# Joins of two chunks in one PSUM tile, over all four 32-row parts, with the Gram products in the same runs (DeltaNet and maxout FFN, one core)

## The chip, the cores and the metric

The kernel runs on one core of one Trainium2 chip. The time is the device time of one execution in microseconds. A core has a matrix engine (TensorE, in the profile PE for matmuls and PEld for weight loads), a vector engine (VectorE, DVE), a scalar engine (ScalarE, ACT), GpSimd (POOL) and a queue that mainly starts DMA transfers (SyncE, SP). Matmuls write to PSUM; DVE and ACT move results from there to SBUF, and here that is called an evacuation.

## What is computed

A delta-rule attention over four batches and eight heads, followed by a feed-forward layer that takes the largest of three products:

```python
k_n = k / (np.linalg.norm(k, axis=-1, keepdims=True) + 1e-06)
for t in range(S):
    kt, vt, bt = (k_n[:, :, t], v[:, :, t], beta[:, :, t, None])
    y[:, :, t] = np.einsum('bhd,bhde->bhe', q[:, :, t], state)
    v_old = np.einsum('bhde,bhd->bhe', state, kt)
    state = state + bt[:, :, :, None] * np.einsum('bhd,bhe->bhde', kt, vt - v_old)
...
x = attn_out.transpose(0, 2, 1, 3).reshape(B * S, H * D)
h = np.maximum(np.maximum(x @ w1, x @ w2), x @ w3)
return h @ w_out
```

B, H, S, D are 4, 8, 768, 48; x is 3072 x 384, w1 to w3 are 384 x 768, w_out is 768 x 384. All inputs are fp32.

## The kernel before

**Chunks, units, groups.** The sequence is cut into 12 chunks of 64 positions. A unit is a chunk of two of the four batches (`n = 2 * c + g`), so there are 24 units; a group is four units, or two chunks, or 512 tokens of the FFN, and there are six. The FFN of group m (`ffn(m)`, L1150) runs while the attention of group m + 1 is made. The order is written by hand: `ffn(m)` is a generator, and after each of its steps `links(m + 1, ...)` (L1348) issues the small pieces of work that the table `LINKS` (L1317) names for this step. A name is a letter and a number: `g` Gram products of a unit, `z` and `j` the two joins of a chunk, `d` transposes for the second join, `k` and `q` products with the state, `u` the new values, `s` the state's update, `y` and `x` outputs, `t` transposed keys and queries, `N` and `L` loads of them. `EARLY_LINKS` is the table for group 1 beside `ffn(0)`, and `FIRST` has the second chunk of group 0. Group 0's first chunk is issued ahead of all (L1283 to L1311).

**Gram products.** `gram(n)` (L395) multiplies keys by keys and queries by keys of a unit into a PSUM tile `p_g`. DVE masks the query part into `pt` (L390), then ACT copies the key part into `at` (L423), and `to_dram` (L427) sends `at` to DRAM with four DMAs, on SP in most groups and on POOL's queue for units 10 and 11.

**Solve.** For each group, `blocks` (L478) loads the 32 x 32 diagonal blocks back (`x_bl`), and `solve` (L498) inverts all of them at once on DVE: after norms (a square root on ACT, L261, into `root_bl`, then small DVE instructions from L262), 31 pairs of DVE instructions (L552, L556) in `x_bl` and `y_bl`. The result goes through DRAM to `ut` (L577, L586).

**Joins.** A chunk of 64 has two blocks of 32. The corner of the inverse is minus the product of the first inverse, the block between and the second inverse. `join_z(c)` (L694) multiplies `at` by the second inverse: for each of 8 heads four matmuls of 32 x 32 by 32 (`TILES`, two partition halves by two units), from rows 32 to 63 and 96 to 127 to PSUM rows 0 to 31 and 64 to 95. Two ACT copies of 32 x 512 bring it to `z` (L705). `join_u(c)` (L707) multiplies the transposed first inverse `t1` by `z`, and two ACT multiplications by -1 write the corner into `ut` (L716). For chunk 0 the heads are split in two batches, with one of four evacuations of `join_u` on DVE (`heads_of`, `negated_of`). `turn_t1` (L615) makes `t1` with DVE transposes. Chunk 0 and 1 have a finer split of the inverse before the joins (`halves_z`, `halves_u`).

**After the joins.** `old_k` subtracts the state's part from v, `new(c)` (L753) multiplies by `ut` into `p_u` and copies to `u`, `step` updates the state `st`, `to_y` makes the output.

**FFN.** A step `hidden` of `ffn(m)` is three matmuls of 128 x 128 by 512 columns into `p_h` (L1161), evacuated by ACT (L1171, L1169) or by DVE as a maximum (L1175); the PSUM tiles of the FFN have two buffers. fp32 matmuls stand in the trace as two records each. The small work shares a PSUM ring of three tiles of two banks (`ps_two`, L83). `weights()` (L221) converts the FFN's weights in `ffn(0)`: three ACT instructions (L238 to L240), one of DVE (L250), one of POOL (L254), with two buffers. `both_layers` (L891) adds matmuls `p_m` in `ffn(1)`.

Of the kernel before, what the change touches and what calls it, by code (L numbers as in the profile page):

```python
# [16 lines left out]
C = 64  # L17
DP = 64
BL = 32
# [4 lines left out]
def kernel(  # L24
# [31 lines left out]
    nc = tc.nc  # L56

    B, H, S, D = q.shape
# [9 lines left out]
    NK, NQ, NU = 8, 3, 2  # L68
# [14 lines left out]
    def ps_two(name):  # L83
        return psum.tile([128, 2, 512], FP32, name=name, tag="two", bufs=3)
# [220 lines left out]
    kqts, ats, pts, xs, at_d = {}, {}, {}, {}, {}  # L305
# [42 lines left out]
    def load_blocks(n, queue=nc.gpsimd):  # L348
        c, g = divmod(n, 2)
        for i in range(2):  # L350
            if n % 4 == 2:
                t = kmore[i].rearrange("p a h d -> p (a h d)")[:, 0 : 2 * TURNED]
                t = t.rearrange("p (b x) -> p b x", b=2)
            else:
                t = work.tile(
                    [128, 2, TURNED], FP32, name="turned", tag="w_bits", bufs=5
                )
            turned[n, i] = t
            nc.gpsimd.memset(t[:, :, TURNED - 48 : TURNED], 0.0)  # L359
# [35 lines left out]
    def gram(n, parts=(0, 1), queues=one_queue, copy=nc.scalar.copy, later=False):  # L395
        kqt, g = kqts[n], n % 2
        p_g = ps_two("p_g")

        whole = len(parts) == 2 and not g
        for j in range(NP):  # L400
            for par in range(2):
                for bb in range(2):
                    kq = kqt[dims(par), j, bb ^ g]
                    for i in (0,) if whole else parts:
                        c0 = j * 128 + i * C
                        nc.tensor.matmul(  # L406
                            p_g[
                                rows(bb ^ (g * i)), par, c0 : c0 + C * (1 + whole)
                            ],
                            kq[:, 0],  # L410
                            kq if whole else kq[:, i],
                        )
        p_v = p_g.rearrange("p two (j i t) -> p two j i t", j=NP, i=2)
        if 1 in parts:
            pt = pts[n] = square("pt")
            if later:
                copy(by_par(pt), p_v[:, :, :, 1])
            else:
                masked(pt, p_v[:, :, :, 1])
        if 0 not in parts:  # L420
            return
        at = ats[n] = square("at")
        copy(by_par(at), p_v[:, :, :, 0])  # L423
        if queues:
            to_dram(n, queues)
# [186 lines left out]
    def block(bb, f=0, n=BL):  # L612
        return slice(C * bb + BL * f, C * bb + BL * f + n)
# [47 lines left out]
    def span(hs):  # L661
        return slice(hs[0], hs[-1] + 1)
# [28 lines left out]
                        -1.0,  # L691
                    )

    def join_z(c):  # L694
        at = [ats.pop(2 * c + g) for g in range(2)]
        z, second = zs[c % NU], ut[c % NU][:, :, :, BL:C]
        for hs, p_v, _ in heads_of(c, "p_z", BL):
            for i, h in enumerate(hs):
                for bb, g in TILES:
                    r = block(bb, 1)  # L700
                    nc.tensor.matmul(
                        p_v[block(bb ^ g), g, i], at[g][r, h, 0:BL], second[r, g, h]
                    )
            for bb in range(2):
                nc.scalar.copy(z[block(bb), :, span(hs)], p_v[block(bb)])  # L705

    def join_u(c):  # L707
        z, t = zs[c % NU], t1[c % NU]
        u12 = ut[c % NU][:, :, :, BL:C]
        for hs, p_v, negate in negated_of(c, "p_j", BL):  # L710
            for i, h in enumerate(hs):
                for bb, g in TILES:
                    r = block(bb ^ g)
                    nc.tensor.matmul(p_v[bb][block(bb), g, i], t[r, g, h], z[r, g, h])  # L714
            for bb in range(2):
                negate[bb](u12[block(bb), :, span(hs)], p_v[bb][block(bb)], -1.0)  # L716


    xts, rhss, qss, us, yts = {}, {}, {}, {}, {}
# [595 lines left out]


    LINKS = {  # L1317
# [3 lines left out]
    }  # L1321
    LAST_LINKS = {**LINKS, 17: "", 19: "X1"}
    EARLY_LINKS = {
# [3 lines left out]
    }  # L1327

# [7 lines left out]

    RECURS = dict(
        z=join_z, j=join_u, k=old_k, q=old_q, u=new, s=step, y=to_y, x=to_x,
        e=halves_z, f=halves_u, d=turn_t1,
    )  # L1340
    MADE = dict(V=load_v, P=prep_values)
    UNIT = dict(
        t=turn, K=load_k, L=lambda n: load_blocks(n, nc.sync),
        g=lambda n: gram(n, queues=(nc.gpsimd,) * 2 if n in (10, 11) else one_queue),
# [129 lines left out]
```

## Time and profile before

| | |
|---|---|
| runs | 510.63, 512.64, 512.75 us; median 512.64 |
| span of the profiled execution, first to last instruction (the page gives no other time of it) | 510.5 us |
| PE busy | 491.1 us (96%) |
| DVE busy | 349.9 us (69%) |
| POOL busy | 192.7 us (38%) |
| ACT busy | 168.7 us (33%) |
| join matmuls, L701 and L714 | 768 records each, 9.1 and 10.4 us |
| their evacuations, L705 and L716 | 26 on ACT; 25 on ACT and one on DVE |
| mean granted TensorE clock | 0.966; 0.57 from 20 to 45 us |

A matmul's record lasts from its start to its modelled end, and matmuls overlap, so busy time is not work at full rate; starts and the chain of waits say more. The granted clock of PE is 1.00 from 55 us on. Busy time by stretch, from the windows of the trace (us, PE, DVE, ACT, POOL busy):

| stretch | what runs | PE | DVE | ACT | POOL |
|---|---|---|---|---|---|
| 20 to 45 | first chunk | 19.17 | 22.14 | 18.62 | 10.62 |
| 55 to 74 | ffn(0), chunk 1 | 16.88 | 17.61 | 14.31 | 9.14 |
| 104 to 116 | ffn(0), group 1 | 12.00 | 7.45 | 11.36 | 9.36 |
| 116 to 131 | ffn(0), group 1 | 13.91 | 14.38 | 4.30 | 4.75 |
| 242 to 315 | ffn(2) | 73.00 | 48.68 | 17.14 | 43.49 |
| 315 to 359 | ffn(3) | 43.91 | 24.71 | 14.45 | 13.41 |

### The profile page before, as it was taken

To read this page: it belongs to the slowest core of one execution; us is meant where nothing else is said; L and a number is where in the kernel's file an instruction comes from. 1 tells how busy PE (TensorE), PEld (TensorE's weight loads), DVE (VectorE), ACT (ScalarE), POOL (GpSimd) and SP (SyncE) were. 2 spreads that over 40 slices of the span, in tenths; PEclk is the share of its full clock that TensorE was granted. 3 is DMA by queue.
4 is the path that set the end of the run, shared out by engine and by line. 5 is a ranking of instruction groups with operands and counts; after the bars stand their busy time and mean duration, and the time that the engine had idled before them with its cause. 6 is when DMAs were issued, how large, how long until landed. Compare 5 with 4: busy or idle time off the path is not lost.

```text
span 510.5 us, 18528 instructions
## 1 busy us (share of the span) xinstructions
PE 491.1 (96%) x8016; PEld 333.1 (65%) x8016; DVE 349.9 (69%) x801; ACT 168.7 (33%) x320; POOL 192.7 (38%) x317
## 2 busy tenths in 40 slices
PE   7778989999999999999999999999999999999996
PEld 6567778756565565665555565555655556998796
DVE  5897799969996430899563987635897455456752
ACT  5585664884422242210252101252101412113210
POOL 7434372783491926670575770503130000000000
PEclk9755999999999999999999999999999999999999
DMA  8938869764055925353675454923343202230001
GB/s 111 192 64 221 194 151 155 195 199 100 5 148 140 175 46 130 99 143 83 144 136 130 120 137 94 174 37 92 80 116 81 44 3 64 54 71 2 0 17 46
DMA packets 106304, 53.49 MB, mean 105 GB/s; under 512 B 89712, under 2 KB 99984, under 8 KB 106224
## 3 DMA queue, kind: packets, MB, share of 16 engines
q1 hardware_dynamic: 94352, 31.35, 30.4%
q0 software_dynamic: 9472, 20.37, 16.4%
q8 instruction: 63, 1.03, 0.9%
q10 hardware_dynamic: 2400, 0.59, 0.6%
q14 instruction: 17, 0.14, 0.1%
HBM read 39.17 MB, written 13.11 MB: 102 GB/s over the span
## 4 chain that ended last, share of the span: by engine, by line
PE 73%; DVE 14%; DMA 5%; ACT 4%; SPq 2%; issue 2%; POOL 0%; DVEq 0%; ACTq 0%; POOLq 0%
PE p_h L1161 26%; PE p_o L1199 13%; PE p_o L960 9%; PE p_e L1102 3%; DVE tmp L552 3%; PE p_g L406 3%; PE p_c L1102 2%; PE p_m L894 2%; PE p_u L759 2%; DMA kmore<-in_k_dram 2%; PE p_k L731 2%; PE p_y L801 2%; DVE y_bl L556 2%; PE p_s L782 2%; PE p_j L714 1%
## 5 line engine op out<-in xcount | busy, mean ns | idle before, releaser
L1161 PE MATMUL p_h<-xt,w_sb 128*128 128x512 f32 (+1 forms) x450 | 187.5, 558 | 0.7 <-ACT xt L827 0.6
L1161 PEld LDWEIGHTS p_h<-xt,w_sb 128*128 128x128 f32 x450 | 82.3, 193 | 68.7 <-issue 61.8
L1199 PE MATMUL p_o<-wo_sb,h 128*128 128x384 f32 x192 | 65.3, 490 | 0.0
L1175 DVE TENSOR_TENSOR h<-h,p_h 128x512 f32<-128x512 f32 (+1 forms) x42 | 25.4, 606 | 53.9 <-PE p_h L1161 52.8
L552 DVE TENSOR_TENSOR tmp<-x_bl,y_bl 128x31 f32<-128x31 f32 (+20 forms) x139 | 51.3, 369 | 4.1
L556 DVE TENSOR_TENSOR y_bl<-y_bl,tmp 128x31 f32<-128x31 f32 (+20 forms) x139 | 48.5, 349 | 4.8
L1199 PEld LDWEIGHTS p_o<-wo_sb,h 128*128 128x128 f32 x192 | 35.7, 190 | 23.2
L364 POOL DMA_DIRECT2D turned<-in_q_dram x72 | 39.1, 551 | 4.3 <-POOL turned L359 2.9
L1205 ACT COPY o_sb<-p_o 128x384 f32<-128x384 f32 x16 | 7.7, 479 | 85.8 <-PE p_o L1199 79.8
L1171 ACT ACTIVATE h<-p_h 128x512 f32<-128x512 f32 x24 | 14.3, 597 | 63.4 <-PE p_h L1161 60.5
L254 POOL TENSOR_TENSOR w_sb<-mant,up 128x384 int32<-128x384 int32 x18 | 19.1, 1059 | 39.3 <-DVE mant L250 39.2
L406 PEld LDWEIGHTS p_g<-kqt 48*64 48x64 f32 x1216 | 24.6, 142 | 9.0 <-issue 6.4
L406 PE MATMUL p_g<-kqt 48*64 48x64 f32 (+1 forms) x1216 | 27.8, 242 | 0.9 <-ACT kqt L335 0.8
L789 DVE TENSOR_TENSOR st<-st,p_s 48x768 f32<-48x768 f32 (+1 forms) x18 | 17.1, 949 | 15.4 <-PE p_s L782 15.2
L120 POOL DMA_DIRECT2D kpad<-in_k_dram x32 | 21.8, 690 | 14.1 <-issue 12.7
L1199 PE MATMUL p_o<-w_sb,xt 128*128 128x384 f32 x72 | 25.2, 486 | 0.0
L139 POOL DMA_DIRECT2D v_t<-in_v_dram x14 | 11.5, 829 | 35.5 <-PE p_u L759 35.5
L390 DVE TENSOR_TENSOR pt<-p_g,mask 128x512 f32<-128x512 f32 x20 | 13.8, 688 | 15.9 <-PE p_g L406 15.8
L287 POOL TENSOR_TENSOR v_t<-v_t,nrm 128x768 f32<-128x768 f32 x12 | 17.9, 1493 | 9.0 <-DVE nrm L281 8.9
L359 POOL MEMSET turned<- 128x96 f32 x18 | 3.3, 192 | 47.6 <-DVE kqt L380 47.6
L759 PEld LDWEIGHTS p_u<-v_t,ut 64*64 64x64 f32 x768 | 13.4, 141 | 10.1 <-issue 7.8
L1199 PEld LDWEIGHTS p_o<-w_sb,xt 128*128 128x128 f32 x72 | 13.7, 190 | 9.5
(212 smaller groups left out, 837.0 us busy)
## 6 DMA issues: line engine op xcount, KB each, us to landing
out_dram<-o_sb SPq DMA_DIRECT2D x40, 96.0 KB
w_bits<-in_moe_w_dram SPq DMA_DIRECT2D x9, 384.0 KB
w_bits<-in_moe_w_dram POOLq DMA_DIRECT2D x9, 384.0 KB, 5.2
turned<-in_q_dram POOLq DMA_DIRECT2D x72, 48.0 KB, 2.9
kpad<-in_k_dram POOLq DMA_DIRECT2D x32, 96.0 KB, 6.1
y_x<-y SPq DMA_DIRECT2D x16, 192.0 KB
qall<-y_x SPq DMA_DIRECT2D x32, 96.0 KB
v_t<-in_v_dram POOLq DMA_DIRECT2D x14, 192.0 KB, 5.0
```

What stands on the lines that cost most here:

```text
L120: queues[bb].dma_start(out=dst[rows(bb ^ g), :, 0:D], in_=src[2 * bb + g, :, c * C : (c + 1) * C, :].rearrange("h p d -> p h d"),)
L254: nc.gpsimd.tensor_tensor(out=dst.bitcast(I32), in0=mant_v.bitcast(I32), in1=up_v, op=ALU.add)
L364: (queue, nc.gpsimd)[i].dma_start(out=t[p0 : p0 + 32, bb, at : at + NP * 2 * D].rearrange("p (j x) -> p j x", j=NP), in_=(k, q)[i][2 * bb ...
L406: nc.tensor.matmul(p_g[rows(bb ^ (g * i)), par, c0 : c0 + C * (1 + whole)], kq[:, 0], kq if whole else kq[:, i],)
L552: nc.vector.tensor_tensor(out=t_v, in0=row.to_broadcast(t_v.shape), in1=column.to_broadcast(t_v.shape), op=ALU.mult,)
L556: nc.vector.tensor_tensor(out=rest, in0=rest, in1=t_v, op=ALU.subtract)
L759: nc.tensor.matmul(p_v[rows(bb ^ g), g, i], ut[c % NU][rows(bb), g, h], rhs[rows(bb), g, h],)
L960: nc.tensor.matmul(to[:, g], a[j][:, 128 * g : 128 * (g + 1)], b[j], start=(start and g == j == 0), stop=(stop and g == 1 and j == PAIRS - 1),
L1102: nc.tensor.matmul(to, w[stays], moves, start=(n == 0), stop=(n == len(terms) - 1))
L1161: nc.tensor.matmul(p_h, w_sb[i][:, t, f * 128 : (f + 1) * 128], xt[:, t, lo : lo + w], start=(t == 0), stop=(t == KT - 1),)
L1175: nc.vector.tensor_tensor(out=h, in0=h, in1=p_h, op=ALU.max)
L1199: nc.tensor.matmul(p_o, stays, moves, start=(n == 0), stop=(n == len(terms) - 1))
```

## The change

Where a group's two chunks are made together (groups 1 to 5), `z0 z1` becomes `b0` and `j0 j1` becomes `c0`: one call for both chunks. It takes one PSUM tile; chunk c has columns 0 to 255 of each bank's part and chunk c + 1 the next 256. All 64 matmuls are issued first, then the evacuations.

In every join, head i now writes PSUM rows 32 * (i % 2) further (`spread`), so that even heads take rows 0 to 31 and 64 to 95, and odd ones 32 to 63 and 96 to 127. The rows that are read stay. An evacuation therefore covers every other head (`parted`): four per chunk and batch where there were two, each of half the size.

In the tables, Gram products move: `g0 g1` stand in step 3 behind `b0` (they were in step 2), and `c0` stands in step 5 ahead of `g2 g3` (the second joins were in step 4). In group 1, `g1` moves from step 14 to 12, `g2` from 16 to 17, and the second join of its second chunk from step 20 to 19.

```diff
-    def join_z(c):
-        at = [ats.pop(2 * c + g) for g in range(2)]
-        z, second = zs[c % NU], ut[c % NU][:, :, :, BL:C]
-        for hs, p_v, _ in heads_of(c, "p_z", BL):
+    def spread(p_v, bb, g, i):
+        return p_v[block(bb, i % 2), g, i // 2]
+
+    def parted(to, bb, hs, par):
+        return to[block(bb), :, hs[0] + par : hs[-1] + 1 : 2]
...
+    def side_by_side(name, cs):
+        p_v = ps_two(name)
+        for i, c in enumerate(cs):
+            part = p_v[:, :, H * BL * i : H * BL * (i + 1)]
+            part = part.rearrange("p g (h x) -> p g h x", x=BL)
+            yield c, range(H), (part, part), (nc.scalar.mul,) * 2
+
+    def join_z(c, both=False):
+        made = []
+        if both:
+            todo = [(n, hs, p_v[0]) for n, hs, p_v, _ in side_by_side("p_z", (c, c + 1))]
+        else:
+            todo = ((c, hs, p_v) for hs, p_v, _ in heads_of(c, "p_z", BL))
...
             for i, h in enumerate(hs):
                 for bb, g in TILES:
                     r = block(bb, 1)
                     nc.tensor.matmul(
-                        p_v[block(bb ^ g), g, i], at[g][r, h, 0:BL], second[r, g, h]
+                        spread(p_v, bb ^ g, g, i), at[g][r, h, 0:BL], second[r, g, h]
                     )
-            for bb in range(2):
-                nc.scalar.copy(z[block(bb), :, span(hs)], p_v[block(bb)])
...
+            made.append((n, hs, p_v))
+            if not both:
+                out_z(*made.pop())
+        for one in made:
+            out_z(*one)
+
+    def out_z(n, hs, p_v):
+        for bb in range(2):
+            for par in range(2):
+                nc.scalar.copy(
+                    parted(zs[n % NU], bb, hs, par),
+                    p_v[block(bb, par), :, 0 : len(hs) // 2],
+                )
+
+    def join_u(c, both=False):
...
-                    nc.tensor.matmul(p_v[bb][block(bb), g, i], t[r, g, h], z[r, g, h])
-            for bb in range(2):
-                negate[bb](u12[block(bb), :, span(hs)], p_v[bb][block(bb)], -1.0)
+                    nc.tensor.matmul(spread(p_v[bb], bb, g, i), t[r, g, h], z[r, g, h])
...
+    def out_u(n, hs, p_v, negate):
+        u12 = ut[n % NU][:, :, :, BL:C]
+        for bb in range(2):
+            for par in range(2):
+                negate[bb](
+                    parted(u12, bb, hs, par),
+                    p_v[bb][block(bb, par), :, 0 : len(hs) // 2],
+                    -1.0,
+                )
...
     LINKS = {
-        0: "k0 q0 t0 L3", 1: "t1", 2: "g0 g1 t2", 3: "z0 z1 d0 d1", 4: "j0 j1 t3 V0",
-        5: "g2 g3 p1", 6: "u0 N0", 7: "V1 N1", 8: "s0 y0 N2", 9: "x0", 10: "k1 q1",
+        0: "k0 q0 t0 L3", 1: "t1", 2: "t2", 3: "b0 g0 g1 d0 d1", 4: "t3 V0",
+        5: "c0 g2 g3 p1", 6: "u0 N0", 7: "V1 N1", 8: "s0 y0 N2", 9: "x0", 10: "k1 q1",
...
     EARLY_LINKS = {
-        9: "k0 q0", 10: "t0", 11: "t1", 12: "g0", 13: "t2", 14: "g1", 15: "t3",
-        16: "g2", 17: "g3", 18: "d0 d1 z0 z1", 19: "j0", 20: "j1 u0", 21: "s0",
+        9: "k0 q0", 10: "t0", 11: "t1", 12: "g0 g1", 13: "t2", 15: "t3",
+        17: "g2 g3", 18: "d0 d1 b0", 19: "c0", 20: "u0", 21: "s0",
...
+        b=lambda c: join_z(c, True), c=lambda c: join_u(c, True),
```

`join_u` is changed in the same way as `join_z`.

More of the change, by code (lines that the diff above doesn't have):

```diff
@@ L692, in halves_u, with spread, parted @@
                     )
-    def join_z(c):
-        at = [ats.pop(2 * c + g) for g in range(2)]
-        z, second = zs[c % NU], ut[c % NU][:, :, :, BL:C]
-        for hs, p_v, _ in heads_of(c, "p_z", BL):
+    def spread(p_v, bb, g, i):
+        return p_v[block(bb, i % 2), g, i // 2]
+    def parted(to, bb, hs, par):
+        return to[block(bb), :, hs[0] + par : hs[-1] + 1 : 2]
+    def spread(p_v, bb, g, i):
+        return p_v[block(bb, i % 2), g, i // 2]
+    def parted(to, bb, hs, par):
+        return to[block(bb), :, hs[0] + par : hs[-1] + 1 : 2]
+    def side_by_side(name, cs):
[10 more added lines that the diff above has]
+            todo = ((c, hs, p_v) for hs, p_v, _ in heads_of(c, "p_z", BL))
+        at_of = {}
+        for n, hs, p_v in todo:
+            if n not in at_of:
+                at_of[n] = [ats.pop(2 * n + g) for g in range(2)]
+            at, second = at_of[n], ut[n % NU][:, :, :, BL:C]
             for i, h in enumerate(hs):
@@ L701, in join_z @@
                     nc.tensor.matmul(
-                        p_v[block(bb ^ g), g, i], at[g][r, h, 0:BL], second[r, g, h]
+                        spread(p_v, bb ^ g, g, i), at[g][r, h, 0:BL], second[r, g, h]
                     )
-            for bb in range(2):
[L705 to L710, printed above, removed]
+            made.append((n, hs, p_v))
[11 more added lines that the diff above has]
+    def join_u(c, both=False):
+        made = []
+        if both:
+            todo = list(side_by_side("p_j", (c, c + 1)))
+        else:
+            todo = ((c, *rest) for rest in negated_of(c, "p_j", BL))
+        for n, hs, p_v, negate in todo:
+            z, t = zs[n % NU], t1[n % NU]
             for i, h in enumerate(hs):
@@ L713, in join_u @@
                     r = block(bb ^ g)
-                    nc.tensor.matmul(p_v[bb][block(bb), g, i], t[r, g, h], z[r, g, h])
-            for bb in range(2):
-                negate[bb](u12[block(bb), :, span(hs)], p_v[bb][block(bb)], -1.0)
+                    nc.tensor.matmul(spread(p_v[bb], bb, g, i), t[r, g, h], z[r, g, h])
+            made.append((n, hs, p_v, negate))
+            if not both:
+                out_u(*made.pop())
+        for one in made:
+            out_u(*one)
+    def out_u(n, hs, p_v, negate):
[7 more added lines that the diff above has]
+                )
     xts, rhss, qss, us, yts = {}, {}, {}, {}, {}
```

## The prediction

> **What bounds the kernel now.** I read the page's chain of work first, then the chain in order of time, and then the timeline of the places where the chain leaves PE.
>
> ```profile
> PE 73%; DVE 14%; DMA 5%; ACT 4%; SPq 2%; issue 2%; POOL 0%; DVEq 0%; ACTq 0%; POOLq 0%
> ```
>
> From about 130 us on the chain is PE without a break, except for 350 to 402 us. Here is the middle of one FFN group, ffn(2), in the chain in order of time (start, length, what; a count holds matmuls and weight loads):
>
> ```profile
> 252.48 2.02 PE p_g L406 x94
> 254.50 2.77 PE p_h L1161 x6
> 257.27 1.28 PE p_z L701 x98
> 258.55 2.77 PE p_h L1161 x6
> 261.32 1.39 PE p_j L714 x99
> 262.71 2.77 PE p_h L1161 x6
> 265.49 2.02 PE p_g L406 x94
> 267.51 2.77 PE p_h L1161 x6
> 270.28 1.08 PE p_u L759 x64
> 271.36 5.35 PE p_h L1161 x12
> ```
>
> Two things are to be seen. Small runs (p_g, p_z, p_j) stand between FFN steps p_h, and a step behind a small run takes 2.77 us, where the second of two joined steps takes 5.35 - 2.77 = 2.58: leaving a small run costs 0.19. Entering one costs about 0.15: p_k behind p_h takes 1.08, p_q of the same size behind p_k 0.93 (both follow in the chain at 283.85 and 284.93). So a small run costs 0.34 us beside its work.
>
> The first chunk is another matter. There the chain passes through each copy of the joins:
>
> ```profile
> 34.53 0.69 PE p_z L701 x32
> ...
> 35.69 0.37 ACT z L705
> ...
> 36.10 1.42 PE p_j L714 x62
> ...
> 37.79 1.14 PE p_u L759 x32
> ...
> 41.37 0.92 ACT y_p L516
> ...
> 44.39 2.93 PE p_h L1161 x6
> ```
>
> And before the last solve, PE itself waits for DVE, which waits for ACT, which waits for a load of Gram blocks (timeline, idle time in brackets):
>
> ```profile
> 352.45 0.26 ACT L261 ACTIVATE root_bl<-x_bl 128x32 f32<-128x32 f32 x1 [1.58 <-DMA x_bl<-at_d]
> ...
> 358.55 0.30 PEld L1161 LDWEIGHTS p_h<-xt,w_sb 128*128 128x128 f32 x2 [0.22 <-DVE h L1175]
> ```
>
> What an evacuation costs stands in the groups by shape:
>
> ```profile
> L716 ACT ACTIVATE ut<-p_j 32x512 f32<-32x512 f32 x22 | 12.9, 587 | 0.7
> ...
> L705 ACT COPY z<-p_z 32x512 f32<-32x512 f32 x22 | 12.7, 576 | 9.5 <-PE p_z L701 9.1
> ...
> L705 ACT COPY z<-p_z 32x256 f32<-32x256 f32 x4 | 1.4, 362 | 0.3 <-PE p_z L701 0.2
> ```
>
> Half the elements cost 362, not 288: (576 - 362)/256 = 0.84 ns per element and 148 ns fixed. Starts of neighbours lie some 25 ns more apart.
>
> **The change, part by part.**
>
> *(a) Evacuations: added.* Each join had two ACT instructions per chunk and batch; it has four of half the size. For a pair of chunks that is 8 x 0.387 = 3.10 us for z where 4 x 0.600 = 2.40 stood, and 8 x 0.398 = 3.18 for u; so +0.70 and +0.78. They also start later: z of the first chunk was copied while the second was multiplied (copies from 258.00, matmuls to 258.48); now all 64 matmuls come first.
>
> *(b) First chunk (not paired), on the chain.* z: 8 copies of 32x128 instead of 4 of 32x256. No 32x128 row exists; the line above gives 148 + 107 = 255 ns, and 16x128 (L688) takes 268, so 0.28 to 0.29 from start to start. u of the first four heads needs z of those: its four copies end 0.37 later (1.14 against 0.77), all eight 0.7 later (2.28 against 1.55). ACT is one queue, so L716 starts behind all eight, 0.7 late, and takes 4 x 0.29 = 1.17 instead of 0.77 for them: p_u at 37.79 moves by 0.7 + 0.4 = 1.1. Behind it stand u, a weight conversion, y, y_p and p_x on ACT and PE, in the chain without slack to 44.39. I take +1.0; bounds +0.5 (DVE's share absorbs some) and +1.3. The same in chunk 1 (57.8 to 62.8 us) is +0.35 twice, but p_j there waits for DVE's transposes until 60.2 and DVE carries the chain: +0.1, bounds 0 and 0.4.
>
> *(c) Four column parts.* No row shows a join that writes four parts; all the tiled groups here use two row and two column parts. Records of a z run start 6 to 7 ns apart within four and wait at the fourth, 32 to 33 ns per four; with 64 columns of weights (p_y) it is 58 per four, with 48 (p_s) 45. So four tiles in turn set the pace, but the second half of each chunk runs in pairs of 16.7 ns, which may be the rate at which instructions arrive. Bounds for 128 records: nothing gained, or half of 128 x 8.3 = 0.53 us per run. The nearest row is the 6.6 ns spacing without a wait: 128 x (8.2 - 6.6) = 0.2; half of a run shows no sign of it, so I take 0.1 per run. One tile instead of two also takes away the waits between chunks (about 0.07 in z, 0.17 in j by the record starts).
> The Trainium skill (TensorE: Matmul & The Clock Gate, Measured speedup vs the span model) reports 16 tiles of 32 x 32 at 10.6 times one tile; by it eight tiles would halve the run, and the total would be near that of rival A. No run here shows it.
>
> *(d) Gram products in the same run.* Two of four small runs vanish per FFN group: 2 x 0.34 saved. But joins (32x32) and Gram (48x64) differ in tile form, and where p_j passes directly to p_u (111.02, last record 111.58, p_u 111.70) the pass costs 0.12, with 0.03 of refill: 0.15 back. Net 0.2 each, 0.4 per group. With (c) a PE-bound group gains 0.4 + 0.24 + 0.2 = 0.8.
>
> *(e) Who waits for the moved steps.* u moves from step 4 to 5 and stands ahead of g2 and g3. In ACT's queue its 8 evacuations now stand ahead of the copy of g2 (L423). Laid out for ffn(3): b0 at 327.6, c0 at 336.1, its evacuations 337.4 to 340.6, copy of g2 done 341.1, where 340.50 stands now: 0.6 late (bounds 0.1 and 1.0). Behind it: 8 issues on SP (340.52 to 344.28), x_bl (345.75, last packet 351.99), root_bl on ACT, the opening of the solve on DVE, and in DVE's queue behind that L1175, for which p_h at 358.55 already waits. So in ffn(3) the gain on PE is lost and the lateness is added: +0.5 (0.1 less, since x_bl shares the DMA with v_t and overlaps less); bounds -0.3 and +1.0. In ffn(2) x_bl landed at 278.49 and DVE was ready for it 0.5 later than ACT: 0.1 of delay, PE's slack behind L1175 is 0.45; of 0.8 I keep 0.35, bounds 0.8 and 0. In ffn(1) x_bl landed at 203.98 for a DVE that took it at 207.68: all of 0.7 to 0.8 kept, I take 0.7 (0.4 if four parts give nothing). Group 5, in ffn(4), has no Gram products; its z waits for ut (0.7 us in two gaps at 400.3), u gains (c): -0.25, bounds -0.6 and 0.
> g0 and g1 come a step later with their 8 issues on SP: those ran 330.06 to 334.73 and would run to about 336.5, before g2's at 341. The transposes d0 d1 stand behind two masks on DVE (1.4 us), and u reads them two steps later, 5 us: nothing. The cover gone, PE would wait for up to 1.4.
>
> *(f) Group 1 in ffn(0).* Here ACT carries the chain: z 106.29 to 108.66, conversion, u, conversion, u, the copy of p_u and root_bl at 115.01, then DVE without a gap to p_u at 130.25. Eight evacuations for four add 1.45. Against it: ACT's conversion at 104.41 waits for POOL's L254 (103.10 to 104.38), which stands behind four at_d issues of g2 (100.67 to 103.09). With g2 in step 17 that L254 goes ahead of them, the conversion can run at about 102, z at 104.7, and root_bl at about 114.85. I take -0.15, bounds -0.6 and +1.4 (POOL holds ACT as before). g1 in step 12 moves 1 us of PE work, not its sum.
> The Trainium skill (TensorEngine Tiling (Array Packing), PSUM Bottleneck) says that packing speeds up TensorE but not the emptying of PSUM, which may become the limit. It speaks against this change; (b) and (f) are where the rows would let it. Were it to hold in (f) too, the sum rises by 1.55.
>
> **Sum** against the profiled execution (span 510.5 us): +1.0 + 0.1 - 0.15 - 0.7 - 0.35 + 0.5 - 0.25 = +0.15. The three runs are 510.63, 512.64 and 512.75; the span is near the lowest and 2.1 below the median. I add the sum to the median: 512.8. With all bounds low it is -2.6 (four parts at the lower half of (c)), with all high +3.7.
>
> **Rivals.** *A, faster: four parts halve the join runs.* For it: all waits within a run come at every fourth record, as with four tiles. Against: pairs of 16.7 ns in the second halves, and ACT gains nothing. Price: seven runs (three z, four u; the last z waits for DMA) x 0.53 = 3.7, six merges x 0.2 = 1.2, and u ends early enough that (e) costs nothing; with +1.1 at the start, -3.8: 508.8.
> *B, slower: ACT's 51 further instructions decide.* Place: group 1, 105 to 115 us, where ACT's queue is the chain; it decides if POOL's L254 doesn't come forward. +1.4 there, +1.2 for the first chunk, +1.0 in ffn(3), +0.3 in chunk 1, -0.4 in ffn(1), 0 in ffn(2) and group 5: +3.5, so 516.1. For it: ACT is busy 11.36 of the 12 us from 104 to 116. Against: ACT stands idle from 102.3 to 104.4.
> *C: four parts do nothing.* Then ffn(1) keeps 0.4, ffn(2) 0, ffn(3) costs 0.8, group 5 gains 0.1, the rest as above: +1.25, 513.9, still no change that can be told.
>
> **Chances.** Some 0.5% (2.6 us) is what a measurement of this kernel can tell. Forecast (with C): 0.62, its own range 510.3 to 515.0; A and other gains beyond 510.1: 0.15; B beyond 515.2: 0.23. So faster 0.15, same 0.62, slower 0.23. Eight in ten: 509.6 to 515.9.
>
> **What would show it.** (a) L705 at 32x256 near 362 ns, 44 of them, and 8 of 32x128. (b) First p_h near 45.4 instead of 44.39. (c) p_z x128 in ffn(2) near 1.0 us; below 0.75 is A. (d) A p_z to p_g pass near 0.15, no p_h between. (e) Last packet of x_bl in ffn(3) later against p_s, PE's wait for L1175 over 0.22. (f) root_bl of group 1 against the first p_h: 70.6 us apart now; 70.2 to 70.8 if I am right, 72 if B. I am wrong if PE waits for a join's evacuation at c0 or u0, or if a shifted POOL instruction lengthens or shortens one of DVE's long ones (2.80 us at 373.39 where its like take 0.42).

## The result

| | before | after |
|---|---|---|
| runs | 510.63, 512.64, 512.75, 514.76 us | 525.08, 525.11, 527.63, 528.83 us |
| median | 512.69 us | 526.37 us |
| span of the profiled execution | 510.5 us | 527.1 us |

The ratio is 1.027, 95% interval 1.023 to 1.032: slower, where no change had been forecast. A time given for a kernel is the median of its executions without those over 1.5% above its fastest one (one is left out in e2 below and one in e10). The 16.6 us between the two profiled spans lie at few places. Counted from p_s to p_s (start of the first weight load, one per group of chunks):

| stretch | before | after | difference |
|---|---|---|---|
| to the first p_z | 34.53 | 36.77 | +2.24 |
| first chunk, p_z to first p_h | 9.86 | 10.68 | +0.82 |
| from there to p_s at 134.8 (ffn(0)) | 90.4 | 89.2 | -1.2 |
| ffn(1) | 69.02 | 68.72 | -0.30 |
| ffn(2) | 72.83 | 77.48 | +4.65 |
| ffn(3) | 72.60 | 78.00 | +5.4 |
| ffn(4) | 68.99 | 73.96 | +4.97 |
| from there to the end | 92.33 | 92.35 | 0 |

The first row lies ahead of all that was changed (the last load of q took 8.04 us there, 6.55 before). ffn(2), ffn(3) and ffn(4) hold 15.0 us of the loss. Here is ffn(2) of after, in the chain in order of time (start, length, what; a count holds matmuls and weight loads):

```profile
256.52 1.29 PE p_z L727 x90
257.82 2.02 PE p_g L406 x94
259.84 5.35 PE p_h L1215 x12
265.18 1.22 PE p_j L755 x80
266.40 0.90 PE p_g L406 x25
267.31 1.76 issue
269.07 2.47 PE p_g L406 x68
271.54 4.93 PE p_h L1215 x6
276.47 1.08 PE p_u L813 x64
```

The order is the one that was planned: p_g behind p_z, p_g behind p_j, two FFN steps at a time. But inside the second p_g PE stands still for 1.76 us, and "issue" says that it waited for nothing that the profile shows: no semaphore, no buffer. Behind the stop an FFN step takes 4.93 us where it took 2.77, at a granted clock of 0.50. The windows of after show the same in ffn(3) (stretch, its length, then busy time and, in brackets, instructions of PE, PEld, DVE, ACT and POOL, then the granted TensorE clock, DMA share and GB/s):

```profile
336.00:340.00 4.00, 1.20 (x72) 1.06 (x62) 0.69 (x1) 2.66 (x7) 0.00 (x0) 1.00 0.48 70
340.00:344.00 4.00, 4.00 (x19) 1.66 (x11) 3.55 (x8) 0.59 (x1) 0.00 (x0) 0.59 0.34 54
```

From 336 to 340 PE is busy for 1.20 of 4 us (the stop is 2.80 us long). From 340 to 344 it is busy throughout, at a granted clock of 0.59. Before, the clock is 1.00 in both stretches. These are all the waits of PE from 135 to 525 us in after (what waited for what: us in total, times, longest):

```profile
PE p_g L406 <- issue: 5.5, 3, 2.8
PE p_h L1215 <- DVE h L1229: 3.0, 1, 3.0
PE p_o L1014 <- DVE y_bl L1162: 0.4, 1, 0.4
```

and all of them in before:

```profile
PE p_o L960 <- DVE y_bl L1108: 0.3, 1, 0.3
```

The waits put down to issue inside p_g are three: 1.76, 2.80 and 0.94 us. Before has none there.

ffn(4) has no Gram products. Its loss is a wait that ends ffn(3)'s solve, again in the chain of after:

```profile
351.62 0.59 ACT at L423
...
357.16 4.98 DMA at_d<-at
...
362.34 4.92 DMA x_bl<-at_d
...
372.37 0.61 DVE h L1229
...
373.03 5.42 PE p_h L1215 x6
```

The copy of g2 stands behind u's eight evacuations, which end at 351.60 (g2's own products were done by 349.57, when DVE's mask of them starts; the stop of 0.94 falls behind them, in g3's). The last of the at_d issues ends at 357.16 and takes 4.98 us to land (1.47 before); x_bl, the opening of the solve and L1229 follow, and PE waits 2.97 us for L1229 where it waited 0.22. The clock is then 0.53 from 371 to 378, and the p_h behind the wait takes 5.42 us instead of 2.77.

What was added by design is of the size that was forecast (groups by shape of after: count, busy us and mean ns):

```profile
L766 ACT ACTIVATE ut<-p_j 32x256 f32<-32x256 f32 x44 | 16.5, 375 | 11.2 <-PE p_j L755 10.7
L739 ACT COPY z<-p_z 32x256 f32<-32x256 f32 x44 | 16.0, 363 | 15.7 <-PE p_z L727 15.1
```

### What the stop could be

One more line of after's page bears on it, among the DMA queues (packets, MB, share):

```profile
q8 instruction: 63, 1.03, 0.8%
```

The queue carries 63 packets of 16,384 bytes. PE has some 16,160 records (weight loads, matmuls and the sequencer's own), and 63 x 256 is 16,128: one packet holds 256 PE instructions of 64 bytes. An fp32 matmul stands as four records (two weight loads, two matmuls), so a packet is 64 small matmuls. In ffn(3) PE stops at 336.42; a packet of this queue runs from 336.58 to 337.91, and PE goes on at 339.22. At the stop in ffn(2) the packet runs from 266.70 to 267.74 and PE goes on at 269.07. So the theories to be told apart were:

- **F**: PE runs out of instructions. A merged run has 64 joins and 48 Gram products, 448 records in some 3.3 us. Before, no run behind 135 us had more than 256 records, and an FFN step (12 records, 2.6 us and more) stood between such runs; one run in ffn(0), p_k with p_y and p_q at 123.47, has 384 in 3.02 us and doesn't stop.
- **A**: the loss is in the evacuations, eight half-size ones per paired join on ACT.
- **X**: the loss starts where u's evacuations stand ahead of the copy of g2 and make x_bl late.

### The profile page after: what moved, and what is told of

It is laid out like the page before. It is cut to its first block, busy times and chain, and to the rows that moved or that the text cites. A ratio compares the mean times of both kernels' runs of the same rounds, so it can differ in the third digit from the quotient of the medians.

```text
span 527.1 us, 18565 instructions
## 1 busy us (share of the span) xinstructions
PE 496.7 (94%) x8016; PEld 335.6 (64%) x8016; DVE 349.6 (66%) x802; ACT 176.7 (34%) x371; POOL 193.0 (37%) x317
## 4 chain that ended last, share of the span: by engine, by line
PE 70%; DVE 8%; DMA 8%; ACT 6%; SPq 4%; issue 3%; ACTq 0%; POOL 0%; DVEq 0%
PE p_h L1215 24%; PE p_o L1253 16%; PE p_o L1014 8%; PE p_e L1156 3%; DMA qall<-in_q_dram 2%; PE p_c L1156 2%; PE p_u L813 2%; PE p_g L406 2%; PE p_y L855 2%; DVE tmp L552 2%; PE p_m L948 1%; DMA ut<-y_d 1%; PE p_k L785 1%; SPq L586 1%; SPq L436 1%
## 5 line engine op out<-in xcount | busy, mean ns | idle before, releaser
L1215 PE MATMUL p_h<-xt,w_sb 128*128 128x512 f32 (+1 forms) x450 | 192.2, 572 | 3.9 <-DVE h L1229 3.0
L1215 PEld LDWEIGHTS p_h<-xt,w_sb 128*128 128x128 f32 x450 | 84.7, 197 | 77.6 <-issue 66.2
L1229 DVE TENSOR_TENSOR h<-h,p_h 128x512 f32<-128x512 f32 (+1 forms) x42 | 25.5, 607 | 60.6 <-PE p_h L1215 58.1
L406 PE MATMUL p_g<-kqt 48*64 48x64 f32 (+1 forms) x1216 | 29.6, 249 | 6.4 <-issue 5.5
L1225 ACT ACTIVATE h<-p_h 128x512 f32<-128x512 f32 x24 | 14.3, 597 | 61.2 <-PE p_h L1215 56.6
L254 POOL TENSOR_TENSOR w_sb<-mant,up 128x384 int32<-128x384 int32 x18 | 18.9, 1050 | 41.1 <-DVE mant L250 31.2
L406 PEld LDWEIGHTS p_g<-kqt 48*64 48x64 f32 x1216 | 26.3, 147 | 10.9 <-issue 8.5
L120 POOL DMA_DIRECT2D kpad<-in_k_dram x32 | 21.9, 692 | 16.6 <-issue 15.2
L739 ACT COPY z<-p_z 32x256 f32<-32x256 f32 (+1 forms) x52 | 18.0, 347 | 16.0 <-PE p_z L727 15.1
L766 ACT ACTIVATE ut<-p_j 32x256 f32<-32x256 f32 (+1 forms) x50 | 18.1, 362 | 11.3 <-PE p_j L755 10.7
```

Of the source, the lines that this page charges most:

```text
L120: queues[bb].dma_start(out=dst[rows(bb ^ g), :, 0:D], in_=src[2 * bb + g, :, c * C : (c + 1) * C, :].rearrange("h p d -> p h d"),)
L254: nc.gpsimd.tensor_tensor(out=dst.bitcast(I32), in0=mant_v.bitcast(I32), in1=up_v, op=ALU.add)
L406: nc.tensor.matmul(p_g[rows(bb ^ (g * i)), par, c0 : c0 + C * (1 + whole)], kq[:, 0], kq if whole else kq[:, i],)
L1215: nc.tensor.matmul(p_h, w_sb[i][:, t, f * 128 : (f + 1) * 128], xt[:, t, lo : lo + w], start=(t == 0), stop=(t == KT - 1),)
L1229: nc.vector.tensor_tensor(out=h, in0=h, in1=p_h, op=ALU.max)
```

## The experiments

All kernels in one table; in the diffs below, entries of the step tables that stay as they are are left out. Until: start of p_s that ends ffn(0)'s group. Groups as above, in us of the profiled execution. Stops: PE's waits put down to issue inside joins, Gram products and p_u behind 135 us.

| kernel | ratio to before, 95% | until | ffn(1) | ffn(2) | ffn(3) | ffn(4) | stops |
|---|---|---|---|---|---|---|---|
| before | 1 | 134.78 | 69.02 | 72.83 | 72.60 | 68.99 | none |
| after | 1.027 (1.023 to 1.032) | 136.62 | 68.72 | 77.48 | 78.00 | 73.96 | 5.5 |
| e1 Gram apart | 1.003 (1.000 to 1.006) | 135.80 | 69.00 | 72.63 | 72.64 | 68.88 | none |
| e2 old joins, merged | 1.022 (1.019 to 1.025) | 134.56 | 68.88 | 75.71 | 78.13 | 68.50 | 4.2 |
| e3 phase at the start | 1.056 (1.051 to 1.062) | 149.42 | 72.10 | 79.47 | 72.74 | 70.37 | 6.7 in p_g |
| e4 Gram first | 1.021 (1.019 to 1.023) | 138.09 | 68.67 | 75.46 | 78.65 | 68.88 | 5.7 |
| e5 half merge | 1.013 (1.008 to 1.018) | 134.93 | 69.58 | 72.66 | 76.63 | 68.77 | 1.6 |
| e6 before, phase | 1.029 (1.025 to 1.033) | 149.09 | 69.08 | 73.18 | 72.65 | 69.36 | 0.3 in p_z |
| e7 pairs only | 1.005 (1.002 to 1.008) | 140.11 | 68.95 | 73.01 | 72.52 | 68.37 | 0.5 in p_j |
| e8 after, phase | 1.052 (1.046 to 1.057) | 152.65 | 74.16 | 78.24 | 72.50 | 68.52 | 7.4 in p_g |
| e9 u with Gram | 1.002 (1.000 to 1.005) | 136.08 | 68.72 | 73.18 | 72.40 | 69.16 | 0.6 |
| e10 Grams together | 1.036 (1.031 to 1.040) | 136.96 | 74.94 | 78.15 | 78.78 | 68.79 | none |

Up to 135 us the executions differ by several us whatever the kernel; the groups behind are read one by one. The run of 384 records in ffn(0) stops too, inside p_q, in the three kernels with dummies ahead of it: 1.16 us in e3, 1.28 in e6, 0.95 in e8.

### e1: Gram products in their own runs again

```diff
-        2: "t2", 3: "b0 g0 g1 d0 d1", 4: "t3 V0",
-        5: "c0 g2 g3 p1",
+        2: "g0 g1 t2", 3: "b0 d0 d1", 4: "c0 t3 V0",
+        5: "g2 g3 p1",
```

> The changed kernel with its Gram products back in runs of their own: the steps 2 to 5 of the table become "g0 g1 t2", "b0 d0 d1", "c0 t3 V0", "g2 g3 p1"; the table for group 1 stays. Theory F (a run of 64 joins and 48 Gram products is longer than the instructions that PE has at hand; it stops inside the run, and its clock is halved for some us behind the stop): no run is longer than 64 small matmuls, so no idle time put down to issue inside p_g, no half clock from 260 to 350 us, and 512.5 to 515.5 us, which leaves the first chunk's +0.8 and the stretched evacuations. Theory A (the eight half-size evacuations per join are the loss, on ACT's queue): they are all still there, so 521 or more. Theory X (the loss starts where u's evacuations stand ahead of the copy of g2 and make x_bl late): c0 is a step earlier, so its loss goes too, but the stalls inside p_g of ffn(2), about 4.7 us with their half clock, have nothing to do with it and the time is 517 or more if anything else than the run's length makes them.

Measured: 515.46 us against 513.73. All eight-fold evacuations are still there, the stops and the half clock behind 135 us are gone, and the three groups are those of before within 0.2 us. PE's waits from 135 to 525 us are:

```profile
PE p_o L1014 <- DVE y_bl L1162: 0.3, 1, 0.3
PE p_z L727 <- DMA ut<-y_d: 0.3, 1, 0.3
```

A falls. What four column parts do without the merge is read here too: p_z takes 1.22 us (1.28 before) and p_j 1.49 (1.39), both to the start of the next p_h.

### e2: the old joins, merged

```diff
-        2: "g0 g1 t2", 3: "z0 z1 d0 d1", 4: "j0 j1 t3 V0",
-        5: "g2 g3 p1",
+        2: "t2", 3: "z0 z1 g0 g1 d0 d1", 4: "t3 V0",
+        5: "j0 j1 g2 g3 p1",
```

The table for group 1 is changed likewise; nothing else of the change is in it.

> The kernel before, with its joins as they were (one PSUM tile per chunk, two row parts, two evacuations per chunk), but in the changed kernel's order: steps 2 to 5 are "t2", "z0 z1 g0 g1 d0 d1", "t3 V0", "j0 j1 g2 g3 p1", and the table for group 1 likewise. Theory F: the merged runs have the same 112 small matmuls, so stops of 1 to 3 us inside them and a half clock behind them come back, and the time is 519 to 526 us. Theory A (evacuations): none of the new ones is here, so within 1 us of the kernel before, 511.5 to 514. Theory X (x_bl late behind u's evacuations): four evacuations instead of eight stand ahead of the copy of g2, about 0.7 us less, and the time is 513 to 516 with no stop inside p_g.

Measured: 524.09 us. The loss is back without a single new evacuation. Its chain in ffn(3):

```profile
332.59 1.32 PE p_g L406 x44
333.91 1.16 issue
335.07 1.02 PE p_g L406 x49
...
344.27 1.44 issue
345.71 0.75 PE p_g L406 x27
346.46 4.47 PE p_h L1161 x6
```

Two stops inside p_g, and behind the second an FFN step of 4.47 us. ffn(4) is whole here (68.50): u's four evacuations ahead of the copy of g2 don't make x_bl late enough to matter.

### e3 and e8: the same program, half a load later

e3 is the changed kernel with 32 dummy matmuls (128 records) at the start; e8 has them in step 22 of ffn(0).

```diff
     busy(6, ident)
+    busy(32, ident[:, 0:32])
```

> The changed kernel with 32 more dummy matmuls of 32 columns at the very start, beside the loads that the first chunk waits for: 128 more PE instruction records ahead of everything else, which is half of one 16 KB instruction load. Theory F with loads in blocks of 256 instructions: every later stop moves by half a block against the program, so the stops fall at other records of p_g or in other groups, and their sum differs: the gap in ffn(3) is not at the 47th p_g record. The time is then anywhere from 514 to 530 us and differs from the changed kernel by more than 2 us. If the stops belong to the program's place (evacuations, PSUM tiles, semaphores), they stay at the same records with the same lengths, and the time is that of the changed kernel within 1.5 us.

> The changed kernel with the same 32 dummy matmuls in step 22 of ffn(0): the phase shift of the dummies at the start, without their cost there. Theory F: behind step 22 the loads stand to the program as with the dummies at the start, so the stops fall where they fell there: in ffn(1) 1.9 and 1.6 us inside p_g, in ffn(2) 3.2 and 1.0, none in the Gram products of ffn(3); the groups take 72, 79.5 and 72.7 us from p_s to p_s where the changed kernel takes 68.7, 77.5 and 78.0. In all 522 to 527. If the stops were drawn anew in each execution, the pattern would not repeat; if they belonged to the place in the program, the pattern would be the changed kernel's.

Measured: 543.12 and 539.62 us, over the 530 and 527 that were expected at most. Of this the dummies themselves are some 10 us (each takes 0.30 us, all writing one PSUM place: in e6 9.70 us for 32), which the expectation for e6 put at 1 to 3. The groups behind tell the theories apart. The stops moved, and moved alike in both kernels: to ffn(1) (weight loads stand still for 1.94 and 1.63 us in e3, 2.30 and 1.63 in e8) and to ffn(2) (3.18 and 1.05; 2.93 and 1.44), at the same records of p_g in both. In ffn(3), the worst group of after, no stop is over 0.6 us, and the group takes 72.74 and 72.50 us. Evacuations, tiles, order and the runs of 112 are the same there. Where a stop falls is set by where the program stands to the 256-record loads, not by the code at that place.

A count over all the traces says the same more sharply. Number PE's records from the start of the program, dummies included. Behind 135 us the ten kernels after, e2 to e9 and e11 have 35 stops of over 0.3 us put down to issue, in p_g, p_j, p_u, p_q and dummies, and every one comes behind a record whose number is 193 more than a multiple of 256.

### e6: the control, phase shifted with short runs

The kernel before with the dummies of e8.

> The kernel before with 32 dummy matmuls of 32 columns (128 records, half a load) in step 22 of ffn(0): a control for the phase. Theory F: runs of 64 with an FFN step of 2.8 us between them leave the load its 4 us wherever its start falls, so the three groups in ffn(1), ffn(2) and ffn(3) take 69.0, 72.8 and 72.6 us from p_s to p_s as before (each within 0.7), and the whole is 1 to 3 us over the kernel before, 513.5 to 516.5. If any change of phase costs, whatever the runs are, then 519 or more.

Measured: 529.58 us, well over what I had expected; the excess is the dummies (9.70 us, with half clock behind them) and the stop in the run of 384, and lies ahead of 149 us. The three groups take 69.08, 73.18 and 72.65 us, all within 0.4 of before. Runs of 256 bear the shift; the one of 384 doesn't. The number for the whole was a miss, the groups were as F had them.

### e5: 88 in a run instead of 112

```diff
-        2: "g0 g1 t2", 3: "z0 z1 d0 d1", 4: "j0 j1 t3 V0",
+        2: "t2", 3: "z0 z1 g0 d0 d1", 4: "j0 j1 g1 t3 V0",
```

> The kernel before, joins as they were, with one Gram unit instead of two behind each of them: steps 2 to 4 are "t2", "z0 z1 g0 d0 d1", "j0 j1 g1 t3 V0", and g2 g3 stay in step 5 by themselves. Runs of 88 small matmuls (352 records) instead of 112 (448). Theory F, with the figure from the traces so far (a 16 KB load is asked for some 300 records before its instructions are needed, and takes about 4 us from there to the first instruction): a stop needs those 300 records to lie in one run, which for 352 records is the case at 52 of 256 positions and for 448 at 148 of 256. So of the six runs of 88 in ffn(1) to ffn(3) none to two have a stop, against four to five of six for the full merge; 512 to 518 us, below the full merge's 524. If the loss came from passing between the two tile forms in one run, and not from the run's length, every merged run would pay, two passes per group as in the full merge, and the time would be 520 or more.

Measured: 519.6 us, 1.6 above the range expected. One of the six runs has a stop, of 1.6 us, with half clock behind it: ffn(3) takes 76.63, the other two groups are those of before within 0.6. So there are fewer stops than with 112, as F had it, but each is dearer than expected, since the clock's part had not been put in.

### e4: Gram products first

```diff
-        5: "c0 g2 g3 p1",
+        5: "g2 g3 c0 p1",
```

> The changed kernel with step 5 as "g2 g3 c0 p1" instead of "c0 g2 g3 p1": the runs stay 112 small matmuls long, but the copies of g2 and g3 stand ahead of u's eight evacuations in ACT's queue. Theory X: x_bl lands earlier by the eight evacuations (3.2 us), PE's wait for L1229 in ffn(3) (2.97 us in the changed kernel) is gone with the half clock behind it, 520 to 522 us if that is all. Theory F: the stops inside the merged runs stay (now partly in p_j), with the half clock behind them, so the time does not come below 517. Theory A: u is ready later against p_u behind it, and the time is 526 or more.

Measured: 524.2 us. The wait for L1229 is gone (ffn(4) 68.88 instead of 73.96), as X had it. The stops stay, now partly in p_j (1.59 us at 349.80), and ffn(2) and ffn(3) with them. So F accounts for the 10 us of ffn(2) and ffn(3), and the 5 us of ffn(4) are a second loss, which goes when the copies of g2 and g3 stand ahead of u's evacuations. That order alone doesn't set its size: with after's order the wait for L1229 is 2.97 us in after, 2.18 in e3 and 0.32 in e8 (ffn(4) 73.96, 70.37 and 68.52). From span to span e4 is 5.0 us below after; the medians are 2.2 apart, since after's other executions were shorter than its profiled one.

### e7: nothing but the paired joins

As e1, and the unpaired joins of chunks 0 and 1 in two parts as before.

```diff
-        return p_v[block(bb, i % 2), g, i // 2]
+        return p_v[block(bb, i % parts), g, i // parts]
```

with `parts` 2 where `both` is set and 1 elsewhere, in the evacuations too.

> The kernel with the Gram products in runs of their own again, and besides with the joins that aren't paired (chunks 0 and 1) in two parts with one evacuation per batch as before; the paired joins keep one PSUM tile and four parts. What is left of the change is just that tile and those parts. The first chunk, first p_z to first p_h: 9.86 us as before instead of 10.12. Paired joins as measured without the merge: p_z 1.22 us instead of 1.28, p_j 1.49 instead of 1.39, so nothing. 511.5 to 514.5 us, no difference from the kernel before that can be told. If four parts gain on the kernel somewhere that the unpaired joins' evacuations took back (rival A of the prediction, halved runs), 510 or less.

Measured: 517.15 us against 513.89, a little slower and over the range expected, with all groups behind 140 us within 0.2 of before or up to 0.6 shorter (ffn(2) has a stop of 0.50 inside p_j). What is lost lies ahead of that: in this execution p_z of group 1 waits three times, 2.5 us together, for the loads of the second inverse around 106 us, and ACT's queue is late behind it. The first chunk takes 9.19 us. Four column parts gain nothing that reaches the end.

### e9 and e10: other merges

e9 puts u0 behind g2 g3; e10 puts all four Gram units in one step.

```diff
-        5: "g2 g3 p1", 6: "u0 N0",
+        5: "g2 g3 u0 p1", 6: "N0",
```

> The kernel before, with u0 (32 matmuls, 128 records, 1.08 us) moved from step 6 behind g2 g3 in step 5: one run of 80 small matmuls, 320 records in 3.1 us, instead of two with an FFN step between. Theory F: 300 of these records take 2.9 us, so a stop of up to 1.1 us, and only at 20 of 256 positions of a load: most likely none. Each group in ffn(1) to ffn(3) loses one entry and exit, 0.2 to 0.35 us: 68.7, 72.5 and 72.3 us from p_s to p_s, unless p_u waits for u's DVE work. 512 to 514.5 us, no difference that can be told from the kernel before; if merging as such costs (a switch between tile forms in a run), the groups take over 73 us and the whole over 515.

```diff
-        2: "g0 g1 t2", 3: "z0 z1 d0 d1", 4: "j0 j1 t3 V0",
-        5: "g2 g3 p1",
+        2: "t2 t3", 3: "z0 z1 d0 d1", 4: "g0 g1 g2 g3 V0",
+        5: "j0 j1 p1",
```

> The kernel before, joins as they were, with the four Gram units of a group in one run: steps 2 to 5 are "t2 t3", "z0 z1 d0 d1", "g0 g1 g2 g3 V0", "j0 j1 p1". The run has 96 small matmuls, 384 records, more than the 352 of the half merge, but in 4.04 us (2.02 us per pair of units in the kernel before) instead of 2.3, since the Gram products are wider. Theory F by time (a load's 4 us against the time that 300 records take): 300 of these records take 3.2 us, so a stop is at most 0.8 us and only where a load falls at the start of the run; each group in ffn(1) to ffn(3) loses one entry and exit, 0.2 to 0.35 us, so 69.0, 72.8 and 72.6 us from p_s to p_s become 68.7, 72.5 and 72.3, each at most 0.8 more: 512 to 514.5 us, no difference that can be told. Theory F by count (a run of more than 300 records stops, whatever its pace): stops of 1.5 to 3 us in about a third of these runs and more than in the half merge's ffn(3), groups of 74 us and more, 515 to 520 us.

e9, measured: 514.69 against 513.75 us, no difference that can be told. ffn(1) and ffn(3) are 0.3 and 0.2 us shorter, as the saved entry has it; ffn(2) has one stop of 0.61 inside p_u and is 0.35 longer.

e10, measured: 533.00 us, for a reason that is neither theory's (PE's waits: us in total, times, longest):

```profile
PE p_g L406 <- ACT at L423: 11.3, 3, 4.2
```

With t3 in step 2 its transposes on DVE wait for a load of keys (to 267.14, and again to 268.42, in ffn(2)), the masks of g0 to g2 stand behind them and behind the transposes for the joins in DVE's queue until 272.72, and the fourth Gram unit waits for a PSUM tile. This says nothing on pace against count. The granted clock was halved in or behind each of the three waits.

### e11 and e12: the limit by itself

Dummy joins that nothing waits for, in ffn(5), which has no other small work. The output isn't touched.

```diff
+    BURSTS = {1: 64, 3: 64, 5: 112, 7: 112, 9: 160, 11: 160, 15: 512}
+
+    def burst(n):
...
+        z, t, p = zs[0], t1[0], ps_two("p_b")
+        for x in range(n):
+            h, (bb, g) = x // 4 % H, TILES[x % 4]
+            r = block(bb ^ g)
+            nc.tensor.matmul(p[block(bb), g, 32 * h : 32 * h + 32], t[r, g, h], z[r, g, h])
...
```

e12 moves four heads at once (128 columns), and its last burst has 256.

> The kernel before with bursts of dummy joins (32 x 32 by 32, four tiles in turn, no evacuation, nothing waits for them) in ffn(5), which has no other small work: 64 and 64, 112 and 112, 160 and 160 matmuls behind steps 1 to 11, and 512 behind step 15, with FFN matmuls of over 3 us between. At the pace of a join run (64 in 1.28 us, 20 ns each) they take 1.3, 2.2, 3.2 and 10.2 us. Theory F: 64 (256 records) never stops; 112 (448 records) takes 2.2 us or, where a load's 300 records fall into it, up to 2.2 us more; 160 (640 records) always has a stop of 1 to 2.5 us; 512 (2048 records, eight loads of 16 KB) runs at the pace of the loads, 2.4 to 4 us each, so 19 to 32 us instead of 10, and the clock is halved behind it. In all 26 us for the bursts and 12 to 31 us of stops: 552 to 572 us. If there is no such limit (the stops come from evacuations, PSUM tiles or the mix of two tile forms), the bursts take 1.3, 2.2, 3.2 and 10.2 us and the whole is 539 to 542.

> The same bursts at the same places, but each matmul with 128 moving columns instead of 32, and 256 in the last burst instead of 512: the same number of instructions over a longer time. No row has this form; by the Gram products (48 in 2.02 us, 42 ns each, 64 to 128 columns) and by p_h (0.92 us for 512 columns) one takes 42 to 230 ns. Theory F by time: 300 records are 75 matmuls, which then take 3.2 us or more where a load needs about 4, so no stop is longer than 0.8 us, the bursts of 64, 112, 160 and 256 take times in proportion to their numbers (each within 10% per matmul), and no half clock follows. Theory F by count: 160 and 256 have stops of 1 to 2.5 us per load as the narrow ones have, so their time per matmul is above that of 64.

| burst | narrow (e11), us | wide (e12), us | wide, ns per matmul |
|---|---|---|---|
| 64 | 1.22, 1.22 | 3.62, 3.63 | 56.6 |
| 112 | 4.43, 4.40 | 6.25, 6.25 | 55.8 |
| 160 | 8.33, 5.70 | 8.87, 8.87 | 55.4 |
| 512 (wide 256) | 26.70 | 14.13 | 55.2 |

e11 took 575.22 us and e12 567.63, against 512.17. The narrow burst of 512, in the chain of e11:

```profile
524.18 2.03 PE p_b L1436 x131
526.22 2.10 issue
528.32 1.93 PE p_b L1436 x128
530.24 1.82 issue
532.06 1.93 PE p_b L1436 x128
```

and the DMA queues of e11 from 524 to 552 us:

```profile
q8 instruction: 8, 0.13, 2.0%
```

PE works for 1.93 us and stops for 1.82, and so on to the end: a stop at every 256th record, one load of 16 KB per period of 3.74 us (3.47 in two of the six periods). Over the run this queue carries 81 packets, and 77 in e12, where before has 63: 18 and 14 more for 4,736 and 3,712 more records, or some 260 each. Nothing waits for these matmuls, they write one tile with one form, and there are no evacuations; the DMA engines are all but idle (busy share 0.05), so the loads aren't held up by other transfers. The clock is 0.56 over this stretch. Of e12's last burst the chain has one line:

```profile
531.30 14.13 PE p_b L1436 x512
```

As many instructions as in half of the narrow burst, no stop, and the clock stays at 1.00. So it is the pace that decides, not the count: the supply is one load per 3.5 to 3.7 us, which is 54 to 58 ns per fp32 matmul (seen at half clock; at full clock e12's 55 ns held for 14 us). A run at 20 ns lives on what is at hand. e11 took 3 us more than the upper end of what was expected: the FFN's own matmuls run at half clock behind the stops, which the expectation had only in words. e11's first stops came 300 to 455 records into a burst.

## Why the prediction was wrong

By its own steps:

- **(a)** The cost of the evacuations was right: 363 ns for 32x256 (44 of them), 257 for 32x128 (8), against 362 and 255; eight z copies took 2.99 to 3.06 us (3.10 forecast).
- **(b)** The first chunk was mis-sized: +1.0 forecast, and +0.27 in e1 and e4, +0.82 in after. Executions differ here by as much (9.19 us in e7, with the old joins there).
- **(c)** 0.1 per run: of the right size, but not in every run (to what follows, p_z is 0.06 shorter in e1 and p_j 0.10 longer; in after, with p_g behind it, p_j is 0.17 shorter). Rival A falls: no run of p_z or p_j was under 1.2 us, where half of one is 0.6 to 0.7.
- **(d)** This is the step that failed: "Net 0.2 each, 0.4 per group. With (c) a PE-bound group gains 0.4 + 0.24 + 0.2 = 0.8." A merge was priced by entry, exit and pass alone, with no bound on the side of a loss. The saving exists (ffn(1) of after is 0.30 shorter, e8's ffn(3) 0.10 although its second p_g takes 0.55 more), but it is bought with the FFN step between the runs, which was the cover for the next instruction load. Before, 268 records took 1.28 + 2.77 = 4.05 us, more than the 3.5 to 3.7 us of a load; merged, 448 records take 3.3. The stops and the half clock behind them are +10 us in ffn(2) and ffn(3), where (d) and (e) together had -0.35 and +0.5. The rows spoke of it: (c) said of 16.7 ns per pair that it "may be the rate at which instructions arrive", and the page lists the instruction queue, but I asked neither how far ahead they are loaded nor what a longer run does to that.
- **(e)** The mechanism was right and the size wrong: the chain from the copy of g2 to L1229 was named, at 0.6 late (bounds 0.1 and 1.0). From the start of its p_g the copy ended 3.82 us later instead of 2.49, 1.3 late, all of it behind u's evacuations. The at_d issues then took 4.93 us for 3.76 (one took 2.07 where its like take up to 0.45) and landed in 4.98 for 1.47; root_bl came 4.4 us late. That cost 5 us in ffn(4) with the clock. With the copies ahead of the evacuations (e4) the wait is gone, but e8 has after's order and waits only 0.32 us: the queue on ACT gives 1.3 of the 4.4, and why the rest varies so stays open. That the late issues meet the load of v_t, issued from 355.91, fits, but was not tried by itself.
- **(f)** L254 came ahead of the four issues (100.99), as forecast. What that gave can't be told: root_bl stood 69.41 us from the first p_h in after, 70.62 in before, but 71.14 in e1 and 73.57 in e4 with the same table for group 1, and 70.69 to 72.76 in e5, e9 and e10 with the old one.
- **The rivals.** B has the right side and the wrong cause: ACT's extra instructions are all in e1, at no loss that decides. C's premise holds nearly: four parts take 0.06 off p_z and at best 0.17 off p_j. That "PE waits for a join's evacuation" and shifted POOL instructions, named as what would make it wrong, were not what did. No part of the sum had a stop inside a run.

The part of the prediction that cited tiling speed-ups (eight tiles halving a run) finds no support in these runs: with four column parts p_z went from 1.28 to 1.22 us, and p_j at best from 1.39 to 1.22.

No version tried beats the kernel before. A merge of 320 records (e9) saves 0.2 to 0.3 us per group and loses it again at one stop, all below what can be told.

## What to carry to other kernels

Before joining runs of small matmuls, count instruction records against time: here PE is fed 256 records per 3.5 to 3.7 us, so a stretch of over some 300 records (the earliest stop in e11) that runs faster than this can stop PE, depending on where it stands to the loads, and slow matmuls between short runs are the cover, not the overhead. Such a stop shows as idle time put down to issue inside a run, at records that lie a multiple of 256 apart and move when unrelated instructions are added ahead; a half clock behind it can cost as much again. A change that merges work on one engine should be priced with a bound for what the removed gap was hiding.

## What the hardware showed beyond expectation

- PE's instructions come during the run as 16 KB packets; 63 of them in each kernel of this size. From the end of a packet to PE's next instruction took 1.3 us at the stop in ffn(2) and the first in ffn(3), 1.5 at the second.
- The granted clock can halve behind short stops, and the length of the stop doesn't decide it: 6.8 us of half clock behind the stop of 1.76, 3.4 behind 2.80 (after), 1.44 (e2) and 1.23 (e4), none behind 0.94 (after), 1.16 (e2), 1.59 (e4), 1.70 (e3) and 2.06 (e8). Where e11 alternates 1.93 us of work and 1.82 of idle it fell to half at the first stop (0.50 from 528 us) and stayed there for 27 us, to the burst's end and 3 us beyond.
- The Trainium skill (TensorE: Matmul & The Clock Gate, What's actually happening) gives a free-running window of 3413 ns; the half-clock stretches behind the stops are 3.41 us long or a multiple of it (6.83 in after, 10.24 and 27.3 in e11), which agrees. Its advice in Why this matters for your kernels, no idle gaps over about 3 us, is too wide for these runs: 1.23 us was enough once.
- 32 matmuls of 128x128 by 32 columns into one PSUM place took 9.70 us, 0.30 each, where a join of 32x32 by 32 took 0.02.
